# Block 0 with its decodings gathered in one place of a step, GpSimd's part moved, and an attention stage without decodings

## The chip, the cores and the metric

The kernel runs on one core of a Trainium2 chip. TensorE (PE in the profile) multiplies matrices into PSUM; VectorE (DVE), ScalarE (ACT) and GpSimd (POOL) work on tiles; SyncE (SP) issues the transfers. Each engine runs its own instructions strictly in the order in which they were written, and waits on semaphores for what other engines make. The metric is the device time of one execution in microseconds (us).

## The reference

```python
def attention(q, k, v):                      # 8 batches, 8 heads, 576 tokens, head size 64
    q_s = softmax(q, axis=-1)                # exp(q - max) / (sum + 1e-9), over the 64
    k_s = softmax(k, axis=2)                 # the same over the 576 tokens
    return q_s @ (k_s^T @ v)

x = attention(q, k, v)                       # as 4608 tokens x 512
h = x @ w_in;  x = (h - tanh(h)) @ w_out     # 512 -> 2048 -> 512
h = x @ w_in2; x = (P(h) / Q(h)) @ w_out2    # P cubic, Q quadratic in |h|, element by element
```

The four weight matrices come as 64-bit floats, the rest as 32-bit floats.

## The kernel before

The 4608 tokens are handled in nine blocks of 512. For each block, 16 steps make the first feed-forward layer: step f multiplies the block's x by slice f of `w_in` (12 matmuls of 128x512 into the PSUM tile `hps`, three for each of four chunks, because every operand is split in a high and a low part: `xh`, `xl`, `wa..h`, `wa..l`), and two steps later the result by slice f of `w_out` (12 matmuls into `acc`, with `gh`, `gl`, `wb..h`, `wb..l`). There are two `hps` tiles. Between the two products lie, in each step: the tanh on ScalarE (`t`), the subtraction h - tanh(h) on VectorE, which in block 0 writes back into `hps`, the cast to the high part `gh` on ScalarE, and the low part `gl`, in block 0 on VectorE. The second layer's weights are prepared beside the blocks 1 to 8, and the last third of the time is the second layer.

In block 0 two other jobs lie beside the steps.

The first is **decoding**. The weights of the first layer arrive as 64-bit floats in 32 pieces of 128x512 (`a` pieces are `w_in`, `b` pieces `w_out`). A piece is opened (`dec_open`: two ScalarE conversions, of line 131 into `e` and of line 133 into `m`, and one VectorE mask of line 134 into `m`), joined (`dec_join`: a VectorE shift of line 146 on `e` and a VectorE instruction of line 147 that puts the two together in `m`), rounded to its high part on ScalarE (`dec_high`, line 154), and its low part is what is left (`dec_low`, line 158, on VectorE or GpSimd). A piece lies in one of three staging tiles `raw` until it is opened, and the next piece's transfer is issued by SyncE when a staging tile is free. One call of `decode` moves several pieces on by one stage each: a low part, a high part, an opening, a joining of the piece opened a call earlier, and one more fetch. Before, a step of block 0 has two such calls, one between `gh` and `gl`, its low part on VectorE, and one behind the step's attention work, its low part on GpSimd; steps 2 and 6 have one.

The second is the **attention of the next block**: of k the column maxima (`kv_max` into `mx`, transposed by TensorE, `kv_top` into `mc`, transposed back, `kv_sub` into `ke`, `kv_exp`), the product with v (`kv_mm`), its scale (`kv_norm`: two small VectorE instructions on `rs`, then the block diagonal `bd` on ScalarE); of q the row maxima (`q_max` into `qm`), the subtraction on GpSimd (`q_sub` into `qe`), `q_exp`, the sums (`q_sum` into `qs`, then a multiplication on GpSimd), the transpose (`q_turn`, copied out as `qh`), the product with `bd` (`q_mm` into `xps`) and the copies into `xr` (`q_out`, four in a row). A table `work` says which step of block 0 runs which function for which of four head pairs. `front` runs a step's plain functions before the tanh, `turn` the TensorE part of the paired ones, and `follow` their second part behind `gl`.

The attention of block 0 itself stands ahead of the steps, as a pipeline of eight stages `s` over the four head pairs; from stage 2 on each has a decoding as well, the last one two. It ends with `xh` cast by ScalarE and `xl` made by VectorE from the product in PSUM (line 679 and 680).

Of the kernel before, what the change touches and what calls it, by code (L numbers as in the profile page):

```python
# [11 lines left out]
U32 = mybir.dt.uint32  # L12
# [6 lines left out]
P = 128  # L19
NB = 512  # L20
# [23 lines left out]
def attention_moe_moe2_kernel(ctx, tc, q, k, v, w1, w2, w3, w4, ca, cb, out):  # L44
# [12 lines left out]
    NPAIR = H // 2  # L57
# [8 lines left out]
    decp = tc.alloc_tile_pool(name="decp", bufs=2, side="right")  # L66
# [7 lines left out]
    PE, ACT, DVE, POOL, SP = nc.tensor, nc.scalar, nc.vector, nc.gpsimd, nc.sync  # L74

    def f32(ap):
        return ap.bitcast(F32)
# [27 lines left out]
    staged, joining, parting = [], [], []  # L105

    def staging():
        return rawp.tile([P, 2 * NB], F32, tag="raw", name="raw")
# [51 lines left out]
    def dec_start():  # L160

        old = [joining.pop()] if joining else []
        if staged:
            piece, t = staged.pop(0)
            if wide:
                joining.append((piece, t, *dec_open(t)))
            else:
                old.append((piece, t, None, t))
        return old

    def dec_end(ph, old, low_on_dve):
        if parting and parting[0][2]:
            dec_low(*parting.pop(0)[:2], low_on_dve)
        for x in parting:
            dec_high(*x[:2])
            x[2] = True
        if wide:
            for _, _, e, m in old:
                dec_join(e, m)
        parting.extend([piece, m, False] for piece, _, _, m in old)  # L180
        fetch_w(ph)

    def decode(ph, low_on_dve):
        dec_end(ph, dec_start(), low_on_dve)

    parked = {}
    UNITS = (1, 5, 2, 6, 7, 4, 3)
# [149 lines left out]
    def split_low(g, gh, gl, eng):  # L339
        eng.tensor_tensor(out=gl, in0=g, in1=f32(gh), op=ALU.subtract)  # L340
# [322 lines left out]
                    )  # L663
        q_state[j, p] = ps

    def q_out(j, p):
        ps = q_state.pop((j, p))
        if j > 0:
            if j > 1 and p % 2 == 0:
                return  # L670
            n = 2 if j > 1 else 1
            for to in range(2):
                for h, r in enumerate(HEADS):
                    ACT.copy(
                        out=xr[r, p + 1 - n:p + 1, to * HALF:(to + 1) * HALF],
                        in_=ps[h][HEADS[to], 0:n * HALF].rearrange("p (c x) -> p c x", c=n),
                    )
        else:
            ACT.copy(out=xh[:, p, :], in_=ps)
# [5 lines left out]
    def front(todo):  # L685
        for fn, args in todo:
            if not isinstance(fn, tuple):
                fn(*args)

    def turn(todo):  # L690

        got = []
        for fn, args in todo:
            if isinstance(fn, tuple):
                fn[0](*args)
                got.append(lambda fn=fn, args=args: fn[1](*args))
        return got

    def follow(after):
        for fn in [late for fn in after for late in [fn()] if late]:  # L700
            fn()

# [4 lines left out]
    def put(s, fn, *args):  # L707
        work[max(s, 0)].append((fn, args))
# [13 lines left out]
    for j in range(1, NBLK):  # L722
        for p in range(NPAIR):
            if j < B:
                s, at = kv_from[j, p], kv_at[j, p]
                steps = (s - 2, s - 1 - (p == 0), s - (p == 0), s + (p > 0), at) if j == 1 else (s - 3, s - 3, s - 1, s, s, s, at)
                for fn, s in zip(KV if j == 1 else KV_LATER, steps):
                    if fn is not kv_max or (j, p) != (1, 0):
                        put(s, fn, j, p)
            s, at = q_from[j, p], q_at[j, p]  # L730
            steps = (s - 1, s, s + 1, s + 2, at - 2, at) if j == 1 else (s - 1, s, s + 1, s + 2, s + 3, s + 5, at)
            for fn, s in zip(Q if j == 1 else Q_LATER, steps):
                if fn is not q_max or (j, p) != (1, 0):
                    put(s, fn, j, p)
        for p in range(2, NPAIR + 2):
            to, before = (j + p // NPAIR, p % NPAIR), (j + (p - 2) // NPAIR, (p - 2) % NPAIR)
            if to in kv_at:
                put(kv_from[before] + 1, load_k, *to)
                put(kv_at[before] + 1, load_v, *to)
            if to in q_at:  # L740
                put(q_from[before] + 2, load_q, *to)

    with tc.manual_schedule():
# [21 lines left out]
        for s in range(NPAIR + 4):  # L765
            def at(k, *fns):

                return [fn(0, s - k) for fn in fns if 0 <= s - k < NPAIR]

            at(1, kv_turn)  # L770
            at(2, kv_back)
            at(3, kv_mm, q_turn)
            at(4, q_mm)
            at(0, kv_max, q_max, q_sub)
            at(1, q_exp)
            at(1, kv_top)
# [165 lines left out]

        STEPS = NBLK * KF
        PAIRS = STEPS // 2
        due = {}
        last = STEPS - KF
        for n in range(STEPS):
            j, f = n // KF, n % KF
            leave = None
            front(work[n])  # L950
            flush()
            hps = first_product(f)
            if f == KF - 1 and j + 1 < NBLK:
# [4 lines left out]
            if n == last + 10:  # L958
# [16 lines left out]
            if n in due:  # L975
# [5 lines left out]
            after = turn(work[n])  # L981
# [12 lines left out]
            split_low(g, gh, gl, POOL if j else DVE)  # L994
            follow(after)
# [81 lines left out]
```

## Time and profile before

| | us |
|---|---|
| median of three executions (1653.03 to 1655.1) | 1654.87 |
| the profiled execution, its own time | 1656.78 |
| its span, first to last instruction | 1655.0 |
| TensorE busy in the span | 1615.7 |
| VectorE / ScalarE / GpSimd busy in the span | 1109.6 / 1024.5 / 1039.2 |
| first matmul of block 0's steps at | 33.66 |
| first matmul that reads block 1's x at | 140.32 |

The profiled execution lies 1.9 us above the median, and 1.8 us of its own time lie around its span. TensorE's busy time counts overlapping and waiting matmuls alike, so that a full row of it does not say that it was fast. Of a stretch, the starts of the instructions tell more: an engine that works through its queue starts each instruction some 0.1 us before the one ahead of it ends.

### The profile page before, as it was taken

To read this page: it belongs to the slowest core of one execution; us is meant where nothing else is said; L and a number is where in the kernel's file an instruction comes from. 1 tells how busy PE (TensorE), PEld (TensorE's weight loads), DVE (VectorE), ACT (ScalarE), POOL (GpSimd) and SP (SyncE) were. 2 spreads that over 40 slices of the span, in tenths; PEclk is the share of its full clock that TensorE was granted. 3 is DMA by queue.
4 is the path that set the end of the run, shared out by engine and by line. 5 is a ranking of instruction groups with operands and counts; after the bars stand their busy time and mean duration, and the time that the engine had idled before them with its cause. 6 is when DMAs were issued, how large, how long until landed. Compare 5 with 4: busy or idle time off the path is not lost.

```text
span 1655.0 us, 26931 instructions
## 1 busy us (share of the span) xinstructions
PE 1615.7 (98%) x9400; PEld 1375.3 (83%) x9400; DVE 1109.6 (67%) x1839; ACT 1024.5 (62%) x1821; POOL 1039.2 (63%) x876
## 2 busy tenths in 40 slices
PE   5999999999999999999999999999999999999998
PEld 3777888888888888887888989898999999999996
DVE  7997656575565556351214787778787777878786
ACT  6785554544545455443326777777777777777775
POOL 4223727374554637373435888888888877888775
PEclk9999999999999999999999999999999999999999
DMA  8662766666474756351487575858585757676640
GB/s 233 192 182 80 217 175 191 169 186 190 147 208 118 227 150 202 104 174 56 142 305 284 178 281 193 285 189 295 190 297 199 276 195 265 206 252 217 208 139 26
DMA packets 250729, 323.76 MB, mean 196 GB/s; under 512 B 119008, under 2 KB 185568, under 8 KB 241376
## 3 DMA queue, kind: packets, MB, share of 16 engines
q1 hardware_dynamic: 250592, 322.03, 60.9%
q8 instruction: 74, 1.21, 0.3%
q14 instruction: 63, 0.52, 0.1%
HBM read 249.04 MB, written 72.93 MB: 195 GB/s over the span
## 4 chain that ended last, share of the span: by engine, by line
PE 82%; DVE 7%; DMA 3%; ACT 3%; issue 2%; SPq 1%; POOL 1%; DVEq 0%; ACTq 0%; POOLq 0%
PE acc L80 14%; PE acc L81 14%; PE acc L82 14%; PE z L871 12%; PE y L871 9%; PE hps L80 6%; PE hps L81 6%; PE hps L82 6%; DVE m L147 1%; DVE m L134 1%; PE kvps L515 1%; PE xps L660 1%; DMA xh<-x2d 1%; DVE e L146 1%; DVE xl L322 0%
## 5 line engine op out<-in xcount | busy, mean ns | idle before, releaser
L340 POOL TENSOR_TENSOR gl<-t,gh 128x512 fp32r<-128x512 f32 x128 | 174.1, 1360 | 301.0 <-ACT gh L336 278.1
L928 POOL TENSOR_TENSOR n<-n,r 128x512 f32<-128x512 f32 x144 | 186.6, 1296 | 98.2 <-ACT r L925 93.0
L986 DVE TENSOR_TENSOR t<-hps,t 128x512 f32<-128x512 f32 x128 | 88.1, 688 | 233.4 <-ACT t L983 233.4
L336 ACT CAST gh<-t 128x512 fp32r<-128x512 f32 x128 | 79.8, 623 | 248.0 <-PE acc L82 140.5
L928 POOL TENSOR_TENSOR n<-n,n 128x512 f32<-128x512 f32 x144 | 186.7, 1296 | 36.1 <-ACT n L912 36.1
L928 POOL TENSOR_TENSOR n<-n,h 128x512 f32<-128x512 f32 x144 | 187.2, 1300 | 9.7 <-DMA xl<-x2d 9.6
L983 ACT ACTIVATE t<-hps 128x512 f32<-128x512 f32 x144 | 86.0, 597 | 121.0 <-PE hps L82 85.3
L882 ACT COPY sums<-z 128x256 f32<-128x256 f32 x144 | 53.8, 374 | 135.0 <-PE z L871 135.0
L908 ACT ACTIVATE n<-h,coef 128x512 f32<-128x512 f32 x144 | 116.7, 810 | 0.3 <-POOL n L928 0.3
L938 DVE CAST gh<-a 128x512 fp32r<-128x512 f32 x144 | 99.6, 692 | 16.5 <-PE z L871 0.9
L941 DVE TENSOR_TENSOR gl<-a,gh 128x512 fp32r<-128x512 f32 x144 | 99.7, 692 | 15.2 <-DVE gh L938 0.5
L934 DVE SCALAR_TENSOR_TENSOR a<-a,n 128x512 f32<-128x512 f32 x144 | 100.0, 695 | 14.3 <-POOL n L928 8.5
L917 DVE SCALAR_TENSOR_TENSOR a<-h,absb,a 128x512 f32<-128x512 f32 x144 | 107.6, 747 | 3.0 <-ACT a L902 2.9
L902 ACT ACTIVATE a<-h,coef 128x512 f32<-128x512 f32 x144 | 100.5, 698 | 2.7 <-DVE gl L941 2.7
L931 DVE SCALAR_TENSOR_TENSOR a<-a,r 128x512 f32<-128x512 f32 x144 | 99.4, 690 | 0.8 <-ACT r L925 0.8
L920 ACT ACTIVATE r<-a,bias_q 128x512 f32<-128x512 f32 x144 | 97.3, 676 | 0.0
L925 ACT ACTIVATE r<-r 128x512 f32<-128x512 f32 x144 | 91.2, 634 | 4.6
L905 ACT ACTIVATE h<-h 128x512 f32<-128x512 f32 x144 | 89.3, 620 | 0.9 <-DMA xh<-x2d 0.8
L889 DVE TENSOR_TENSOR h<-y,sums 128x256 f32<-128x256 f32 x72 | 30.6, 425 | 58.6 <-PE y L871 58.6
L893 DVE TENSOR_TENSOR h<-y,top 128x512 f32<-128x512 f32 x72 | 49.7, 691 | 27.4 <-ACT top L882 27.1
L613 POOL TENSOR_TENSOR qe<-qe,qs 128x512 f32<-128x512 f32 x36 | 40.6, 1128 | 38.7 <-DVE qs L612 35.4
L80 PE MATMUL acc<-wb3h,gh 128*128 128x512 f32 x144 | 57.0, 396 | 2.9 <-DVE gh L938 2.9
(296 smaller groups left out, 5114.2 us busy)
## 6 DMA issues: line engine op xcount, KB each, us to landing
u<-x2d SPq DMA_DIRECT2D x78, 256.0 KB, 5.5
raw<-in_moe_w_in_dram SPq DMA_DIRECT2D x32, 512.0 KB, 4.8
raw<-in_moe_w_out_dram SPq DMA_DIRECT2D x32, 512.0 KB, 4.1
x2d<-raw SPq DMA_DIRECT2D x64, 256.0 KB, 3.5
x2d<-xr SPq DMA_DIRECT2D x56, 256.0 KB, 3.8
wa0h<-wa0d SPq DMA_DIRECT2D x9, 1024.0 KB, 5.0
wa1h<-wa2d SPq DMA_DIRECT2D x9, 1024.0 KB, 5.0
wa2h<-wa4d SPq DMA_DIRECT2D x9, 1024.0 KB, 5.2
```

Source lines behind the costliest of these rows:

```text
L80: PE.matmul(o, lhi, rhi, start=start, stop=False)
L81: PE.matmul(o, lhi, rlo, start=False, stop=False)
L82: PE.matmul(o, llo, rhi, start=False, stop=stop)
L340: eng.tensor_tensor(out=gl, in0=g, in1=f32(gh), op=ALU.subtract)
L871: PE.matmul(o, w, x[:, xc], start=m in (1, 5) and c == k == 0, stop=c == 1 and k == 2, skip_group_check=True,)
L902: ACT.activation(out=new(t, "a", ps_a), in_=t["h"], func=AF.Abs, scale=b0)
L908: ACT.activation(out=new(t, "n1"), in_=t["h"], func=AF.Identity, scale=a3, bias=a2)
L917: DVE.scalar_tensor_tensor(out=t["a"], in0=t["h2"], scalar=b1, in1=t["a"], op0=ALU.mult, op1=ALU.add)
L928: return lambda t: POOL.tensor_tensor(out=t[a], in0=t[a], in1=t[b], op=op)
L934: DVE.scalar_tensor_tensor(out=t["a"], in0=t["a"], scalar=2.0, in1=t["n0"], op0=ALU.subtract, op1=ALU.mult)
L938: DVE.tensor_copy(out=t["g"][0], in_=t["a"])
L941: DVE.tensor_tensor(out=t["g"][1], in0=t["a"], in1=f32(t["g"][0]), op=ALU.subtract)
```

## The change

It does five things.

1. `dec_start`, `dec_end` and the lists `joining` and `parting` go. A piece now moves through the lists `staged`, `opened`, `joined` and `ready` by four functions: `opens(n)`, `joins(n)`, `highs(n)` and `lows(engines)`.
2. A step of block 0 has one place for VectorE's decoding, behind `gl`: the low part of one piece, two openings, the joining of whatever is opened, and one high part. The other high part stands on ScalarE right behind the tanh, and GpSimd's low part behind that.
3. The attention functions that use VectorE and GpSimd (`BESIDE`) stand between the subtraction and `gl`, and the exponentials (`CLOSING`) at the step's end instead of ahead of its tanh. `kv_top` and the `kv_sub` of a turn move on to the next step.
4. In the attention of block 0, stages 2 to 4 have a decoding; stages 5 to 7 only a few single stages of one. The results of the head pairs 0 and 1 are cast to `xh` by VectorE.
5. The transfers of k for block 1 stand a step later.

```diff
+    def opens(n):
+        for _ in range(min(n, len(staged))):
+            piece, t = staged.pop(0)
+            if wide:
+                opened.append((piece, *dec_open(t)))
...
+            fetch_w(0)
+    def joins(n):
+        for _ in range(min(n, len(opened))):
+            piece, e, m = opened.pop(0)
+            if wide:
                 dec_join(e, m)
+            joined.append((piece, m))
+    def highs(n):
+        for _ in range(min(n, len(joined))):
+            dec_high(*joined[0])
+            ready.append(joined.pop(0))
+    def lows(*engines):
+        for eng in engines[:len(ready)]:
+            dec_low(*ready.pop(0), eng is DVE)
...
+    BESIDE = (kv_max, kv_squares, kv_join, kv_sub, q_max, q_sub, q_sum, q_squares)
+    CLOSING = (kv_exp, q_exp)
...
-            if s < NPAIR + 3:
-                if s >= 2:
-                    decode(0, False)
-                at(5, q_out)
-            else:
+            if 2 <= s <= NPAIR:
+                decode()
+            elif s == NPAIR + 1:
+                lows(POOL)
+                q_out(0, 0, DVE)
+            elif s == NPAIR + 2:
+                highs(1)
+                q_out(0, 1, DVE)
+                lows(POOL)
+            elif s == NPAIR + 3:
+                q_out(0, 2)
+                q_out(0, 3)
+                joins(1)
+                highs(1)
                 kv_max(1, 0)
                 q_max(1, 0)
-                at(5, q_out)
-                at(4, q_out)
-                decode(0, False)
-                decode(0, False)
+                opens(2)
+                lows(DVE)
+                joins(1)
+                fetch_w(0)
...
             ACT.activation(out=t, in_=hps, func=AF.Tanh)
 
             g = t if j else hps
             DVE.tensor_tensor(out=g, in0=hps, in1=t, op=ALU.subtract)
-            ph_w, turns = None, 0
-            if j == 0:
-                ph_w, turns = 0, 1 if f in (2, 6) else 2
+            if not j:
+                highs(2)
+                first = ready[0:1]
+                del ready[0:1]
+                lows(POOL, POOL)
+                follow(beside)
+                only(work[n], BESIDE)
+                if n in due:
+                    due.pop(n)()
+                after = turn(work[n])
+                beside = [x for x in after if x[0] in (kv_top, kv_sub)]
+                after = [x for x in after if x not in beside]
             gh, gl = split_high(g)
             due[n + LAG1] = lambda a=(j, f, gh, gl): second_product1(*a)
-            if turns:
-                decode(ph_w, True)
             split_low(g, gh, gl, POOL if j else DVE)
+            if not j:
+                for x in first:
+                    dec_low(*x, True)
+                opens(2)
+                joins(3)
+                highs(1)
             follow(after)
+            if not j:
+                only(work[n], CLOSING)
             if leave:
                 leave()
-            if turns > 1:
-                decode(ph_w, False)
```

What this does to the order on the engines is seen at three places. The first is VectorE in step 4 of block 0, from its subtraction (`hps`) on; before:

```order
L986 TENSOR_TENSOR hps<-hps,t 128x512
L134 TENSOR_SCALAR m<-raw 128x512
L158 TENSOR_TENSOR wa1l<-m,wa1h 128x512
L146 TENSOR_SCALAR e<-e 128x512
L147 ISA m<-e,m 128x1024
L340 TENSOR_TENSOR gl<-hps,gh 128x512
L520 TENSOR_SCALAR rs<-xps 128x1
L521 RECIPROCAL rs<-rs 128x1
L474 TENSOR_REDUCE mc<-xps 128x1
L134 TENSOR_SCALAR m<-raw 128x512
L146 TENSOR_SCALAR e<-e 128x512
L147 ISA m<-e,m 128x1024
```

and now:

```order
L1011 TENSOR_TENSOR hps<-hps,t 128x512
L348 TENSOR_TENSOR gl<-hps,gh 128x512
L158 TENSOR_TENSOR wa1l<-m,wa1h 128x512
L134 TENSOR_SCALAR m<-raw 128x512 x2
L146 TENSOR_SCALAR e<-e 128x512
L147 ISA m<-e,m 128x1024
L146 TENSOR_SCALAR e<-e 128x512
L147 ISA m<-e,m 128x1024
L528 TENSOR_SCALAR rs<-xps 128x1
L529 RECIPROCAL rs<-rs 128x1
L1011 TENSOR_TENSOR hps<-hps,t 128x512
```

Nothing now stands between the subtraction and `gl`; both masks of line 134 follow the low part of line 158, the two shift-and-join pairs stand one behind the other, `rs` is last before the next subtraction, and `mc` went into step 5.

The second is ScalarE in the same step, from one tanh (`t`) to the next; before:

```order
L983 ACTIVATE t<-hps 128x512
L336 CAST gh<-hps 128x512
L131 ACTIVATE e<-raw 128x512
L133 ACTIVATE m<-raw 128x512
L154 CAST wb1h<-m 128x512
L527 ACTIVATE bd_114<-xps,rs 128x64
L131 ACTIVATE e<-raw 128x512
L133 ACTIVATE m<-raw 128x512
L154 CAST wa1h<-m 128x512
L983 ACTIVATE t<-hps 128x512
```

and now:

```order
L1008 ACTIVATE t<-hps 128x512
L154 CAST wb1h<-m 128x512
L344 CAST gh<-hps 128x512
L131 ACTIVATE e<-raw 128x512
L133 ACTIVATE m<-raw 128x512
L131 ACTIVATE e<-raw 128x512
L133 ACTIVATE m<-raw 128x512
L154 CAST wa1h<-m 128x512
L535 ACTIVATE bd_114<-xps,rs 128x64
L613 ACTIVATE qe<-qe 128x512
L1008 ACTIVATE t<-hps 128x512
```

One high part (`wb1h`) moved from the middle to right behind the tanh; the other (`wa1h`) stands behind all four conversions; `bd` and the exponential of `qe` stand between it and the next tanh.

The third is VectorE in the last stages of block 0's own attention, from the scale (`rs`) of head pair 2 on; before:

```order
L520 TENSOR_SCALAR rs<-kvps 128x1
L521 RECIPROCAL rs<-rs 128x1
L134 TENSOR_SCALAR m<-raw 128x512
L146 TENSOR_SCALAR e<-e 128x512
L147 ISA m<-e,m 128x1024
L680 TENSOR_TENSOR xl<-xps,xh 128x512
L520 TENSOR_SCALAR rs<-kvps 128x1
L521 RECIPROCAL rs<-rs 128x1
L134 TENSOR_SCALAR m<-raw 128x512
L146 TENSOR_SCALAR e<-e 128x512
L147 ISA m<-e,m 128x1024
L680 TENSOR_TENSOR xl<-xps,xh 128x512
```

and now:

```order
L528 TENSOR_SCALAR rs<-kvps 128x1
L529 RECIPROCAL rs<-rs 128x1
L687 CAST xh<-xps 128x512
L688 TENSOR_TENSOR xl<-xps,xh 128x512
L528 TENSOR_SCALAR rs<-kvps 128x1
L529 RECIPROCAL rs<-rs 128x1
L687 CAST xh<-xps 128x512
L688 TENSOR_TENSOR xl<-xps,xh 128x512 x3
L146 TENSOR_SCALAR e<-e 128x512
L147 ISA m<-e,m 128x1024
```

Two whole decodings (masks, shifts and joins) went from here, and two casts to `xh` came in.

## Rows read from the trace of the kernel before

**Rows 1.** Busy time by engine (instructions) from step 0's tanh to step 15's.

```profile
40.49:141.85 101.36, 92.32 (x515) 71.27 (x514) 92.44 (x172) 76.16 (x145) 26.82 (x22) 0.98 0.53 161
```

**Rows 2.** Groups of VectorE in that stretch: busy us, mean ns | idle before.

```profile
L134 DVE TENSOR_SCALAR m<-raw 128x512 uint16<-128x512 uint16 x25 | 17.7, 710 | 0.0
L146 DVE TENSOR_SCALAR e<-e 128x512 uint32<-128x512 uint32 x27 | 13.8, 510 | 0.0
...
L485 DVE TENSOR_TENSOR ke<-kt,kvps 128x640 f32<-128x640 f32 x4 | 3.2, 811 | 0.0
L610 DVE TENSOR_REDUCE qs<-qe 128x8 f32<-128x512 f32 x4 | 2.7, 678 | 0.0
...
L590 DVE TENSOR_REDUCE qm<-qr 128x8 f32<-128x512 f32 x4 | 2.6, 662 | 0.0
```

**Rows 3.** Timeline of VectorE in step 12: start us, us.

```profile
120.10 0.47 DVE L134 TENSOR_SCALAR m<-raw 128x512 uint16<-128x512 uint16 x1
120.44 0.67 DVE L158 TENSOR_TENSOR wb3l<-m,wb3h 128x512 fp32r<-128x512 f32 x1
121.03 0.42 DVE L146 TENSOR_SCALAR e<-e 128x512 uint32<-128x512 uint32 x1
121.49 0.69 DVE L147 CUSTOM_DVE_ANT_0 m<-e,m 128x1024 uint16<-128x1024 uint16 x1
122.10 0.68 DVE L340 TENSOR_TENSOR gl<-hps,gh 128x512 fp32r<-128x512 f32 x1
122.70 1.56 DVE L134 TENSOR_SCALAR m<-raw 128x512 uint16<-128x512 uint16 x1
```

**Rows 4.** Timeline of ScalarE in step 12 (between brackets: idle before, releaser).

```profile
118.87 0.58 ACT L983 ACTIVATE t<-hps 128x512 f32<-128x512 f32 x1
...
121.97 0.60 ACT L154 CAST wa3h<-m 128x512 fp32r<-128x512 f32 x1
122.47 0.59 ACT L624 COPY qh<-qps 128x512 f32<-128x512 f32 x1
```

**Rows 5.** Timeline of VectorE in step 15.

```profile
144.11 0.69 DVE L340 TENSOR_TENSOR gl<-hps,gh 128x512 fp32r<-128x512 f32 x1 [0.71 <-ACT gh L336]
```

**Rows 6.** Groups of ScalarE in the stretch of rows 1.

```profile
L674 ACT COPY xr<-xps 64x256 f32<-64x256 f32 x16 | 5.9, 366 | 0.2
L605 ACT ACTIVATE qe<-qe 128x512 f32<-128x512 f32 x5 | 3.1, 628 | 0.0
L495 ACT ACTIVATE ke<-ke 128x640 f32<-128x640 f32 x4 | 3.0, 744 | 0.0
...
L527 ACT ACTIVATE bd<-xps,rs 128x64 f32<-128x64 f32 x4 | 1.3, 314 | 0.7 <-DVE rs L521 0.6
```

**Rows 7.** One line's VectorE instructions: duration ns min/median/max, first and last start (L457).

```profile
L457 DVE TENSOR_TENSOR mx<-mx,kt x3: 292/293/1016, 59.0 to 99.7; 128x128 f32<-128x128 f32 x3
```

**Rows 8.** The same for L225, a later line, in the blocks behind.

```profile
L225 DVE TENSOR_TENSOR m<-m,e x21: 405/682/1772, 179.7 to 418.8; 128x512 fp32r<-128x512 f32 x18, 128x256 fp32r<-128x256 f32 x3
```

**Rows 9.** Timeline of GpSimd beside the first of rows 7.

```profile
58.84 1.05 POOL L613 TENSOR_TENSOR qe<-qe,qs 128x512 f32<-128x512 f32 x1 [6.47 <-DVE qs L612]
```

**Rows 10.** Timeline of VectorE: the subtractions of steps 2 and 13.

```profile
54.37 0.70 DVE L986 TENSOR_TENSOR hps<-hps,t 128x512 f32<-128x512 f32 x1
...
127.77 0.69 DVE L986 TENSOR_TENSOR hps<-hps,t 128x512 f32<-128x512 f32 x1
```

**Rows 11.** Timeline of TensorE: last value product of the first attention.

```profile
26.84 0.80 PE L515 MATMUL kvps<-vt,ke 128*64 128x65 f32 x20 [1.42 <-ACT ke L495]
```

**Rows 12.** Timeline of TensorE at the end of block 0.

```profile
133.30 0.50 PE L80 MATMUL hps<-xh,wa3h 128*128 128x512 f32 x1
...
138.65 0.39 PE L82 MATMUL acc<-gh,wb3l 128*128 128x512 f32 x1
...
144.90 0.53 PE L82 MATMUL hps<-xh,wa0l 128*128 128x512 f32 x1
```

**Rows 13.** Waits of TensorE from 145 to 1100 us, the longest group.

```profile
PE z L871 <- ACT sums L882: 2.4, 2, 1.9
```

More of the change, by code (lines that the diff above doesn't have):

```diff
@@ L104, in attention_moe_moe2_kernel @@
     ]
-    staged, joining, parting = [], [], []
+    staged, opened, joined, ready = [], [], [], []
     def staging():
@@ L158, in dec_low, with decode @@
         (DVE if on_dve else POOL).tensor_tensor(out=lo, in0=f32(m), in1=f32(hi), op=ALU.subtract)
-    def dec_start():
-        old = [joining.pop()] if joining else []
-        if staged:
+    def opens(n):
+        for _ in range(min(n, len(staged))):
             piece, t = staged.pop(0)
             if wide:
-                joining.append((piece, t, *dec_open(t)))
+                opened.append((piece, *dec_open(t)))
             else:
[L168 to L178, printed above, removed]
-                dec_join(e, m)
[L180 to L184, printed above, removed]
+                m = decp.tile([P, NB], U32, tag="m", name="m", bufs=4)
+                POOL.tensor_copy(out=f32(m), in_=t)
+                opened.append((piece, None, m))
+            fetch_w(0)
[3 more added lines that the diff above has]
+            if wide:
+                dec_join(e, m)
+            joined.append((piece, m))
[6 more added lines that the diff above has]
+            dec_low(*ready.pop(0), eng is DVE)
+    def decode():
+        n, r = len(opened), len(ready)
+        opens(1)
+        lows(*[POOL] * r)
+        highs(1)
+        joins(n)
     parked = {}
@@ L664, in q_mm, with q_out @@
         q_state[j, p] = ps
-    def q_out(j, p):
+    def q_out(j, p, eng=ACT):
         ps = q_state.pop((j, p))
@@ L678, in q_out @@
         else:
-            ACT.copy(out=xh[:, p, :], in_=ps)
+            (ACT.copy if eng is ACT else DVE.tensor_copy)(out=xh[:, p, :], in_=ps)
             DVE.tensor_tensor(out=xl[:, p, :], in0=ps, in1=f32(xh[:, p, :]), op=ALU.subtract)
@@ L683, in attention_moe_moe2_kernel, with front, only @@
     Q_LATER = (q_max, q_sub, q_exp, q_sum, q_squares, q_fetch, (q_mm, q_out))
-    def front(todo):
+    BESIDE = (kv_max, kv_squares, kv_join, kv_sub, q_max, q_sub, q_sum, q_squares)
+    CLOSING = (kv_exp, q_exp)
+    def front(todo, leave=()):
         for fn, args in todo:
-            if not isinstance(fn, tuple):
+            if not isinstance(fn, tuple) and fn not in leave:
+                fn(*args)
+    def only(todo, these):
+        for fn, args in todo:
+            if fn in these:
                 fn(*args)
@@ L695, in turn @@
                 fn[0](*args)
-                got.append(lambda fn=fn, args=args: fn[1](*args))
+                got.append((fn[1], args))
         return got
     def follow(after):
-        for fn in [late for fn in after for late in [fn()] if late]:
-            fn()
+        for fn, args in after:
+            fn(*args)
     work = {s: [] for s in range(NBLK * KF)}
@@ L737, in attention_moe_moe2_kernel @@
             if to in kv_at:
-                put(kv_from[before] + 1, load_k, *to)
+                put(kv_from[before] + (2 if before[0] == 1 else 1), load_k, *to)
                 put(kv_at[before] + 1, load_v, *to)
@@ L944, in attention_moe_moe2_kernel @@
         PAIRS = STEPS // 2
-        due = {}
+        due, beside = {}, []
         last = STEPS - KF
@@ L949, in attention_moe_moe2_kernel @@
             leave = None
-            front(work[n])
+            front(work[n], () if j else BESIDE + CLOSING)
             flush()
@@ L974, in attention_moe_moe2_kernel @@
                     load_unit(0, u)
-            if n in due:
+            if j and n in due:
                 leave = due.pop(n)()
@@ L980, in attention_moe_moe2_kernel @@
                 ring(f // 4 - 1)
-            after = turn(work[n])
+            after = turn(work[n]) if j else []
             t = gp.tile([P, NB], F32, tag="t", name="t", bufs=1)
@@ L986, in attention_moe_moe2_kernel @@
             DVE.tensor_tensor(out=g, in0=hps, in1=t, op=ALU.subtract)
-            ph_w, turns = None, 0
-            if j == 0:
-                ph_w, turns = 0, 1 if f in (2, 6) else 2
+            if not j:
[10 more added lines that the diff above has]
+                after = [x for x in after if x not in beside]
             gh, gl = split_high(g)
             due[n + LAG1] = lambda a=(j, f, gh, gl): second_product1(*a)
-            if turns:
-                decode(ph_w, True)
             split_low(g, gh, gl, POOL if j else DVE)
+            if not j:
[3 more added lines that the diff above has]
+                joins(3)
+                highs(1)
             follow(after)
+            if not j:
+                only(work[n], CLOSING)
             if leave:
                 leave()
-            if turns > 1:
-                decode(ph_w, False)
             if n == KF:
```

## The prediction

> **What bounds it now.** I first asked where a microsecond counts. From 145 us on TensorE hardly waits: the longest group in 955 us is 2.4 us [rows 13]. So whatever block 0 gains or loses until the first product of block 1 ends (its last matmul starts at 144.90 [rows 12]) reaches the end one for one, and nothing behind it changes its order.
>
> In block 0 the stretch from the first tanh to the last takes 101.36 us for 15 steps. VectorE is busy for 92.44 of them, ScalarE for 76.16, GpSimd for 26.82 [rows 1]. TensorE's 92.32 are no measure: at the pace of 133.30 to 138.65 (23 starts in 5.35 us, 0.23 each [rows 12]) the 24 matmuls of a step are worth 5.6 us, 84 for 15 steps, and the attention products some 11 more. VectorE is therefore what sets the step. Part of its time is lost beside GpSimd: a mask takes 0.47 us alone [rows 3] and 0.71 on average, a shift 0.42 and 0.51 [rows 2, 3]; the mask at 122.70 took 1.56. That is 25 x 0.24 + 27 x 0.09 = 8.4 us. The step's own time, from the subtraction of step 2 (54.37) to that of step 13 (127.77) [rows 10], is 73.4 / 11 = 6.67 us.
>
> **The change, part by part.**
>
> *Ahead of the steps.* The last value product of the first attention ends at 27.64 [rows 11], and nothing ahead of it changes. From there the new order is: scale and block diagonal of pair 3, 1.8 us (two small VectorE instructions, four ScalarE ones); its product, 1.0; `xh`, 0.6; `xl`, 0.7; then shift and join of the third piece (0.46 + 0.73 [rows 3]) to 33.1; its high part, 0.5 [rows 4]; four conversions on ScalarE at some 0.6 each, 2.4; tanh and hand-over, 0.62. The first subtraction comes at 36.6. The 1.8, 1.0, 0.6, 0.7 and 2.4 are estimates from instructions of the same size (0.59 to 0.69 for 512 columns [rows 3, 4]). Step 0 joins three pieces and takes 6.5, step 1 takes 5.6 by the chain below, and I add 0.5 because TensorE's transpose for the k maxima now waits for `mc` of step 1: the subtraction of step 2 at 49.2 instead of 54.37, **5.2 us gained**. It costs two pieces that block 0 has to decode in addition.
>
> *A step.* Now the order matters. ScalarE's last high part stands behind all conversions and waits for the first join of the same step; behind it stand the step's closing work and then the tanh, for which VectorE's next subtraction waits. That is a closed chain, with these links from start to start: subtraction to `gl` 1.40 (0.69 and 0.71 of waiting for `gh`, as in step 15 [rows 5], because nothing fills the gap any more); `gl` to the low part 0.60, low part to mask 0.59, two masks 0.69, shift to join 0.46, join to its end and hand-over 0.73 [rows 3]; high part 0.50, tanh with hand-over 0.62 [rows 4]. Sum 5.59, and 61.5 for steps 2 to 12. The second shift and join lie beside the high part and the tanh and cost nothing; without that cover they would cost 1.1 a step. ScalarE's four conversions lie beside `gl`, the low part and the masks.
>
> Attention on VectorE lies between the subtraction and `gl` and is covered up to 0.8 us. Start to start I take 0.72 for `ke`, 0.60 for `qm`, 1.03 for `qs` with its two small ones (their durations in [rows 2], less 0.1 where the next does not depend on it), and as estimates 0.66 for `mx` (0.29 for its second instruction [rows 7], more for the first, which is twice as wide) and 0.34 for `mc`. What exceeds 0.8 is 0.52 in step 2, 0.89 in 3, 1.17 in 5 and 8, 0.58 in 6 and 9, 0.57 in 11: 5.5.
>
> The closing work on ScalarE lies on the chain in full: in steps 2 to 12 four `ke` and four `qe` exponentials, four `qh` copies, eight `xr` copies and three `bd`: 11.7 us by their durations [rows 4, 6], 10.2 from start to start. Before it was hidden: ScalarE had 25 us to spare in the stretch [rows 1] and VectorE did not wait for it. In step 4 `bd` also waits for `rs`, which is behind the second join: 0.9.
>
> So steps 2 to 12 take 61.5 + 5.5 + 11.1 = 78.1 us without any collision, against 73.4: the 8.4 us of collisions go, and 4.7 more than them come in as waits.
>
> *GpSimd beside VectorE.* GpSimd's low part now starts some 0.5 us behind the subtraction and ends 1.3 us later, beside the subtraction and `gl`, which read PSUM. But behind it, in its queue, stand the multiplication of `qe` behind `qs` (1.05 [rows 9]) and the subtraction behind `qm` (1.1 to 1.2, as its neighbour), and these now run beside VectorE's low part, which has both operands in SBUF, or beside `mx`. The trace has VectorE's low part never beside GpSimd, so I bound it: 0 if it doesn't mind, and the rest of the GpSimd instruction if it must wait. For the second speak two near rows: `mx`, which also has two SBUF operands, took 1.016 instead of 0.292 beside the multiplication at 58.84 [rows 7, 9], and L225, a subtraction of the low part's shape, took up to 1.772 against 0.682 [rows 8]. I take the waiting: 0.7 in step 2, 0.5 in 3, 1.05 in 5 and 8, 0.5 in 6, 9 and 11: 4.8, and 0.7 in step 13. The Trainium skill, "SBUF — State Buffer", section "Who interferes with whom", says that a VectorE instruction with two SBUF inputs contends with a GpSimd instruction that reads SBUF, while a reduction never does. The trace agrees in the 1.016 and 1.772 us; by that rule the sum is the one with the 4.8, and sums and `gl` are safe company but the k maxima of block 1 (two `tensor_tensor`) are not.
>
> *The end of block 0.* Step 13 has 2.5 us of attention ahead of `gl`; then low part, one mask, shift, join, high part, four `xr` copies, `bd`: the block diagonal of pair 3 is ready 8.1 us behind the subtraction (0.6 + 2.5 + 0.60 + 0.59 + 0.35 + 0.46 + 0.73 + 0.50 + 1.5 + 0.3). Its product (1.0) and three products of 12 matmuls (35 starts, 8.1) follow without a gap: 17.3 to the last matmul of block 1's first product. Before it was 144.90 - 127.77 = 17.1, with a later wait for `xh` and slow matmuls in it. So +0.2, or +0.9 with GpSimd in the way.
>
> *Sum.* The subtraction of step 13 comes at 49.2 + 78.1 + 4.8 = 132.1 instead of 127.77, +4.3; with the end +5.2, rounded **+5 us**. Without collisions it is -0.3. On the profiled execution's own 1656.78 us this gives 1661.8; on the median, 1.9 lower, **1659.9 us**.
>
> **The rivals.**
>
> *No collisions, the rest as worked out* (or an early start that is 4 us better than I think): -0.3, 1654.6. For it speaks that the order was laid so that GpSimd's low part meets only PSUM readers; against it the queue behind that low part.
>
> *Faster: VectorE keeps its queue full.* Its own work in a step is 0.60 + 0.60 + 0.59 + 0.69 + 2 x 1.08 = 4.6 us; with some 12 of attention and `rs` steps 2 to 12 are 64 us, 14 below the chain. If half of the closing work and of the wait for `gh` is covered after all (conversions finished ahead of time, so that ScalarE reaches high part and tanh early), 7 us come off: 1653 with the collisions, 1648 without. It decides at 6.67 us a step on average: below that, less the 0.5 a step that the early start is worth, the change gains. Against it: the high part stands behind the join in ScalarE's order, and can't be early.
>
> *Slower still: TensorE at a lower rate.* It now stands for a transpose that waits for `mc` in four steps, and ahead of pair 3's product. Block 1's first product before shows the price: it took from 140.32 (the table above) to 144.90 [rows 12], 4.6 us, where 11 starts of 0.23 are 2.6; some 2 us, its wait for `xl` included. If that falls on the three products at the end, +2 to +4: 1662 to 1664.
>
> *The change misses its point.* If the freed collisions are simply taken over by the next queue, without waits, nothing moves: that lies in the first rival's range.
>
> **Chances.** Forecast and lower rate together 0.47, the first rival with its neighbours 0.31, faster 0.22. A difference of 0.2% (3.3 us) is about what a measurement of this kernel tells from none; the forecast lies outside it, the first rival inside. The likeliest case alone is 1657 to 1663; the range, 1648 to 1665, takes in the faster rival without collisions and one slow product with the collisions.
>
> **What would show it.** Right: the first subtraction at 36 to 37 us and TensorE's first product of block 0 some 3 us earlier; ScalarE idle before line 154's high part, released by the join; VectorE idle before the subtraction, released by the tanh, by 10 us or more in block 0, most in steps with `xr` copies; masks at 0.47, but low parts and `mx` of over 1 us. Wrong: a step below 6.2 us on average, a low part of 0.67 us beside GpSimd, or TensorE without waits in block 0.

## The result, and the profile after

The changed kernel takes 1663.26 us in the median of four executions (1662.6 to 1664.21), the kernel before beside it 1654.47: 0.55% slower, ratio 1.0055 with a 95% interval of 1.0037 to 1.0072, +8.8 us. The forecast was 1659.9, the range 1648 to 1665.

The two profiled executions differ by less: spans of 1661.0 and 1655.0. The tanh of step 17 starts at 159.05 instead of 150.99, 8.06 us later; at step 143, the last one, the difference is still 8.41. Most of the missing 2.4 us was lost by the profiled execution of before, later on. Windows of before (first) and after (second) at the passage to the second layer (columns: us, busy us of PE, PEld, DVE, ACT and POOL, granted TensorE clock, DMA share, GB/s):

```profile
860.00:900.00 40.00, 36.60 (x203) 31.98 (x202) 13.43 (x22) 19.68 (x35) 16.05 (x14) 0.96 0.82 312
```

```profile
868.00:908.00 40.00, 36.61 (x211) 31.80 (x211) 13.00 (x21) 20.19 (x37) 15.78 (x14) 1.00 0.82 301
```

Before had 0.96 of the clock in that stretch, after has all of it, which by estimate is worth 40 x 0.04 = 1.6 us of the 2.4; the distance between the two kernels' equal ScalarE instructions falls from 8.42 us (starts 896.74 and 905.16) to 6.91 (908.02 and 914.93) there. Where the rest went was not looked into. So the change's own cost is 8 to 9 us, as the medians say, and all of it arises in block 0.

The stretch from step 0's tanh to step 15's, and eight microseconds near its end, after:

```profile
35.86:148.81 112.95, 93.57 (x502) 72.95 (x501) 92.33 (x177) 81.88 (x150) 28.44 (x23) 0.91 0.51 154
```

```profile
140.00:148.00 8.00, 5.47 (x29) 3.93 (x30) 5.32 (x11) 6.51 (x15) 0.00 (x0) 0.79 0.13 33
```

[rows 1] had 101.36 us with VectorE busy for 92.44. It is busy for the same 92.33 now, but in 112.95 us: 4.6 of the 11.6 that were added are the earlier start, 7.0 the later end, and the whole is waiting. The subtractions of steps 2 and 13 after, to be held against those of [rows 10]:

```profile
49.98 0.70 DVE L1011 TENSOR_TENSOR hps<-hps,t 128x512 f32<-128x512 f32 x1
...
133.93 0.70 DVE L1011 TENSOR_TENSOR hps<-hps,t 128x512 f32<-128x512 f32 x1 [1.13 <-ACT t L1008]
```

VectorE's groups in that stretch (busy us, mean ns, idle before):

```profile
L134 DVE TENSOR_SCALAR m<-raw 128x512 uint16<-128x512 uint16 x27 | 11.6, 485 | 0.0
L146 DVE TENSOR_SCALAR e<-e 128x512 uint32<-128x512 uint32 x28 | 11.6, 415 | 0.0
L1011 DVE TENSOR_TENSOR hps<-hps,t 128x512 f32<-128x512 f32 x15 | 10.5, 699 | 10.2 <-ACT t L1008 10.2
L348 DVE TENSOR_TENSOR gl<-hps,gh 128x512 fp32r<-128x512 f32 x15 | 10.2, 682 | 3.2 <-ACT gh L344 3.1
L158 DVE TENSOR_TENSOR wa3l<-m,wa3h 128x512 fp32r<-128x512 f32 x4 | 3.8, 959 | 0.0
L465 DVE TENSOR_TENSOR mx<-mx,kt 128x128 f32<-128x128 f32 x3 | 3.1, 1017 | 0.1
```

The masks fell from 710 to 485 ns and the shifts from 510 to 415 [rows 2]: those collisions are gone, but for one pair of masks in step 1 that took 1.64 us. In their place VectorE waits 10.2 us for the tanh and 3.1 for `gh`, and the collisions that are left moved to the low parts and `mx`.

The chain behind the 10.2 us, in step 7. ScalarE (first fence) and VectorE (second):

```profile
92.91 0.62 ACT L154 CAST wa2h<-m 128x512 fp32r<-128x512 f32 x1 [0.76 <-DVE m L147]
93.43 1.51 ACT L682 COPY xr<-xps 64x256 f32<-64x256 f32 x4
94.98 0.32 ACT L535 ACTIVATE bd<-xps,rs 128x64 f32<-128x64 f32 x1
95.19 0.62 ACT L613 ACTIVATE qe<-qe 128x512 f32<-128x512 f32 x1
95.71 0.59 ACT L1008 ACTIVATE t<-hps 128x512 f32<-128x512 f32 x1
```

```profile
88.33 0.70 DVE L1011 TENSOR_TENSOR hps<-hps,t 128x512 f32<-128x512 f32 x1 [0.64 <-ACT t L1008]
89.73 0.69 DVE L348 TENSOR_TENSOR gl<-hps,gh 128x512 fp32r<-128x512 f32 x1 [0.71 <-ACT gh L344]
...
92.18 0.69 DVE L147 CUSTOM_DVE_ANT_0 m<-e,m 128x1024 uint16<-128x1024 uint16 x1
...
96.33 0.70 DVE L1011 TENSOR_TENSOR hps<-hps,t 128x512 f32<-128x512 f32 x1 [1.39 <-ACT t L1008]
```

The join that starts at 92.18 releases the high part (`wa2h`); behind it stand four copies, `bd`, an exponential and the tanh, and VectorE's subtraction waits 1.39 us for that. The largest waits of ScalarE for joins, step 0 to 16 (total us, times, longest):

```profile
ACT wa1h L154 <- DVE m L147: 6.5, 4, 3.0
ACT wa2h L154 <- DVE m L147: 6.4, 4, 1.9
ACT wa3h L154 <- DVE m L147: 5.9, 4, 2.4
ACT wb3h L154 <- DVE m L147: 3.8, 1, 3.8
```

### The profile page after: what moved, and what is told of

It reads as the page before. It is cut to its first block, busy times and chain, and to the rows that moved or that the text cites. A ratio compares the mean times of both kernels' runs of the same rounds, so it can differ in the third digit from the quotient of the medians.

```text
span 1661.0 us, 26916 instructions
## 1 busy us (share of the span) xinstructions
PE 1615.2 (97%) x9400; PEld 1375.7 (83%) x9400; DVE 1105.3 (67%) x1842; ACT 1025.4 (62%) x1819; POOL 1038.5 (63%) x875
## 4 chain that ended last, share of the span: by engine, by line
PE 86%; DVE 5%; DMA 4%; ACT 3%; issue 1%; SPq 1%; POOL 0%; DVEq 0%; ACTq 0%; POOLq 0%
PE acc L80 14%; PE acc L81 14%; PE acc L82 14%; PE z L896 12%; PE y L896 9%; PE hps L80 7%; PE hps L81 7%; PE hps L82 7%; DMA u<-x2d 1%; PE kvps L523 1%; PE xps L668 1%; DVE m L147 1%; DMA xh<-x2d 1%; DMA qr<-in_q_dram 0%; DMA raw<-in_moe_w_out_dram 0%
```

## The experiments

Three theories were set against each other. A: the closed chain of join, high part, closing work, tanh and subtraction. B: GpSimd beside VectorE. C: the stages ahead and what they hand on, TensorE's delays with them. One table holds all runs; "steps 2 to 12" runs from the subtraction of step 2 to that of step 13, "end" from there to the tanh of step 17, all from the profiled execution. The first three steps vary by up to 1.7 us between kernels that are the same there, so the medians decide. Each ratio is to the kernel before as it was measured beside that run, with medians from 1653.77 to 1654.47.

| kernel | subtr. 2 | subtr. 13 | steps 2 to 12 | end | median | ratio to before (95%) |
|---|---|---|---|---|---|---|
| before | 54.37 | 127.77 | 73.40 | 23.22 | 1654.47 | |
| after | 49.98 | 133.93 | 83.95 | 25.12 | 1663.26 | 1.0055 (1.0037 to 1.0072) |
| e1_high_free | 52.12 | 130.22 | 78.10 | 22.20 | 1655.81 | 1.0007 (0.9997 to 1.0018) |
| e2_high_last | 50.15 | 131.93 | 81.78 | 22.41 | 1656.37 | 1.0014 (1.0003 to 1.0025) |
| e3_stages_alone | 49.29 | 127.06 | 77.77 | 23.18 | 1652.13 | 0.9988 (0.9975 to 1.0001) |
| e4_steps_alone | 54.59 | 138.75 | 84.16 | 20.87 | 1663.35 | 1.0054 (1.0036 to 1.0072) |
| e5_no_q_gpsimd | 49.78 | 132.43 | 82.65 | 23.73 | 1660.56 | 1.0040 (1.0025 to 1.0055) |
| e6_masks_in_gap | 51.60 | 130.79 | 79.19 | 21.94 | 1656.01 | 1.0008 (0.9998 to 1.0018) |
| e7_rs_early_xr_split | 52.30 | 128.47 | 76.17 | 22.68 | 1652.91 | 0.9992 (0.9982 to 1.0003) |
| e8_lows_on_gpsimd | 52.75 | 131.90 | 79.15 | 22.39 | 1656.54 | 1.0015 (1.0004 to 1.0025) |
| e9_top_in_step_0 | 50.14 | 133.88 | 83.74 | 25.07 | 1662.34 | 1.0053 (1.0040 to 1.0066) |
| e10_rs_early_no_masks | 52.22 | 127.40 | 75.18 | 22.95 | 1652.23 | 0.9991 (0.9983 to 1.0000) |
| e11_best | 47.42 | 121.31 | 73.89 | 23.73 | 1647.01 | 0.9963 (0.9950 to 0.9976) |
| e12_end_high_last | 50.76 | 135.86 | 85.10 | 22.45 | 1660.29 | 1.0042 (1.0029 to 1.0055) |

**e1, the link cut.**

```diff
-                highs(2)
-                first = ready[0:1]
-                del ready[0:1]
+                highs(len(joined) - 1)
...
             gh, gl = split_high(g)
+            if not j:
+                highs(1)
...
-                for x in first:
-                    dec_low(*x, True)
+                lows(DVE)
                 opens(2)
                 joins(3)
-                highs(1)
```

> The changed kernel with one edit: no high part stands at a step's end; both stand behind the next tanh, one ahead of gh (its low part on GpSimd), one behind gh (its low part on VectorE). ScalarE then never waits for a join with the tanh behind it. Theory A (the closed chain join, high part, closing work, tanh, subtraction): the link is cut, VectorE's own order sets the step, 5.6 us and the attention beyond 0.8; steps 2 to 12 fall from 83.95 to 70 to 75 us and the time to 1650 to 1655. Theory B (GpSimd's instructions beside VectorE's make the steps long): those stay, 1661 to 1664. Theory C (the loss lies in the stages ahead and in the work that they hand on): 1661 to 1664.

Steps 2 to 12 fell by 5.85 us, the end by 2.9, the time by 7.4, although the subtraction of step 2 came 2.1 us later. B and C can't be the whole, A holds, but the steps fell by half of what it expected, and the time lies 0.8 us above its range. VectorE in e1, from the end of step 7 to the end of step 8:

```profile
96.37 0.70 DVE L1011 TENSOR_TENSOR hps<-hps,t 128x512 f32<-128x512 f32 x1 [1.39 <-ACT t L1008]
...
102.55 0.69 DVE L147 CUSTOM_DVE_ANT_0 m<-e,m 128x1024 uint16<-128x1024 uint16 x1
103.16 0.69 DVE L1011 TENSOR_TENSOR hps<-hps,t 128x512 f32<-128x512 f32 x1
```

Step 8 ends without a wait: VectorE's own order is the limit there, at 6.79 us, only 0.59 below the chain's 7.38. Step 7 still ends with 1.39 us of waiting, at 7.35 us instead of 8.00: there ScalarE's own row of conversions, copies, `bd` and exponential is almost as long as the chain was (from `gh` at 89.80 to the tanh at 95.75 it pauses for 0.28 us only).

**e2, the closing work off the chain.** The one line `highs(1)` stands behind `only(work[n], CLOSING)`.

> The changed kernel with one line moved: the step's last high part stands behind the closing work, not ahead of it. The join still releases the high part and the tanh still stands behind it; only the closing work (11.1 us in steps 2 to 12) leaves the chain and goes into the time in which ScalarE waits for the join. Theory A: steps 2 to 12 fall by 7 to 10 us, to 74 to 77, and the time to 1653 to 1656. Theories B and C: no change, 1661 to 1664.

The time is 0.4 us above A's range, 6.9 below the changed kernel; steps 2 to 12 are not as A said (-2.2 instead of -7 to -10). The rows and the median don't add up here: the profiled execution, at 1658.71, lies 2.3 us above the median. ScalarE's largest group of waits says what took the place, against 0.9 us in the changed kernel:

```profile
ACT bd L535 <- DVE rs L529: 6.6, 4, 2.7
```

`rs` stands on VectorE behind both joins, so in steps 4, 7, 10 and 13 `bd` waits for it, with the high part and the tanh behind. The end gave 2.7 us, of which e12 tells more.

**e3 and e4, one part alone.** e3 puts the new stages ahead of before's steps (with two decodings in every step), e4 before's stages ahead of the new steps; the lists of pieces are handed over in between.

> One part alone: the first attention's new last stages, with the steps of the kernel before, which now have two decodings in steps 2 and 6 too (the two that left the stages). Theory A: the subtraction of step 0 comes at some 36.5 instead of 41.36, the steps keep 6.67 us, the two additional decodings cost some 2 us each; 0 to 2 us faster than the kernel before, 1653 to 1655. Theory C: the stages are the loss, 1658 or more.

> The other part alone: the steps of the changed kernel behind the first attention's old stages. Theory A: the first subtraction comes at 41.4, the steps take 7.6 us each as in the changed kernel, the last ones a little less because two pieces fewer are left; 1664 to 1668, slower than both kernels. Theory C: 1655 to 1658.

The steps are the whole loss: alone they cost as much as the change. The stages alone bring 2 us in the median, which is not clear of noise (0.9975 to 1.0001). In the profile they are 5.1 us ahead at step 2, and 0.7 are left at step 13, because the two pieces that the stages no longer decode cost 2.6 us in step 2 and 1.7 in step 6. With the new steps they bring nothing, since after and e4 have the same time: 4.8 us ahead at step 13 are given back in an end that is 4.25 longer. After has a mask, a shift and a join in step 13 that e4 has done before, and e4's TensorE has its full clock there (1.00 from 140 to 148 us).

**e5, GpSimd's q instructions left out.**

```diff
-        POOL.tensor_tensor(out=t, in0=t, in1=sm.to_broadcast([P, 8, D]), op=ALU.mult)
+        if j != 1:
+            POOL.tensor_tensor(out=t, in0=t, in1=sm.to_broadcast([P, 8, D]), op=ALU.mult)
```

and the same for the subtraction, with the exponential reading `qr`.

> The changed kernel without GpSimd's two instructions on the q of block 1 (the subtraction of the row maxima and the multiplication by the inverse sums are left out; everything else, VectorE's part too, stays). This is the price of GpSimd beside VectorE in the changed kernel. Theory A (the chain, with 4.8 us of collisions in steps 2 to 12 as predicted): 3 to 5 us less than the changed kernel, 1658 to 1660. Theory B (the collisions are the loss): 8 us or more less, 1655 or below.

2.7 us less, just short of A's range: B falls, and taking these instructions away brings back less than the 4.8 forecast. In step 6 of after, GpSimd (first) and VectorE (second), and VectorE in the same step of e5 (third):

```profile
82.11 1.22 POOL L603 TENSOR_TENSOR qe<-qr,qm 128x512 f32<-128x512 f32 x1
```

```profile
82.46 1.02 DVE L465 TENSOR_TENSOR mx<-mx,kt 128x128 f32<-128x128 f32 x1
```

```profile
81.89 0.29 DVE L465 TENSOR_TENSOR mx<-mx,kt 128x128 f32<-128x128 f32 x1
```

Each collision is there and goes with its GpSimd instruction: steps 3, 6, 9 and 11 get 0.6 to 1.0 us shorter, 2.9 together. But steps 2 and 12 got 0.6 and 0.9 longer (there `gh` waits 1.64 and 1.26 us for TensorE's `acc`), so steps 2 to 12 gain 1.3 in all. The other 1.4 lie in the end, where TensorE kept its clock: `bd` starts 8.53 us behind the subtraction of step 13 in both kernels, but block 1's first product ends 17.66 behind it in e5 and 19.19 in the changed kernel.

**e6, e7, e10: the next limits behind the chain.** e6 is e1 with the two masks in the 0.71 us in which VectorE waits for `gh`; e7 has in addition `rs` behind `gl` and two of the four `xr` copies on VectorE; e10 is e7 with the masks back.

> As e1_high_free, and the two masks stand between the subtraction and gl, where VectorE waits 0.71 us for gh in steps without attention. If VectorE's order now sets the step, steps 4, 7, 10 and the first ones get up to 0.7 us shorter each, 1 to 4 us in all: 1652 to 1655. If ScalarE's order sets just those steps (its row of conversions, xr copies, bd and the exponential of qe in steps 7 and 10), nothing but 1 us: 1655 to 1656.

> As e6_masks_in_gap, and what keeps ScalarE from the tanh in steps 4, 7, 10 and 13 is made shorter: rs stands behind gl instead of behind the joins, and VectorE makes two of the four xr copies. Steps 7 and 10 of e1_high_free had 1.39 us of waiting for the tanh each. Expected: 2 to 5 us less than e6_masks_in_gap, 1648 to 1652. If those steps are set by something else, no change.

> As e7_rs_early_xr_split, with the masks back behind the low part, so that they don't meet GpSimd's low part (pairs of 1.28 to 1.64 us there, 0.80 in e1_high_free) and VectorE waits again 0.7 us for gh in steps without attention. Theory A: both are worth about the same, within 1.5 us of e7_rs_early_xr_split, 1651.5 to 1654.5, and 2 to 4 less than e1_high_free. Theory B: the masks' collisions were the larger part, 2 us or more less than e7_rs_early_xr_split.

e6 gained nothing, 1656.01 against 1655.81, at the edge of the second case of its expectation; e7 gained 3.1 us as expected but lies 0.9 above its stated range, e10 came as expected, and the two are equal. Why masks in the gap bring nothing stands in GpSimd's (first) and VectorE's rows (second) of e7 in step 7:

```profile
87.51 1.57 POOL L158 TENSOR_TENSOR wa2l<-m,wa2h 128x512 fp32r<-128x512 f32 x1 [4.39 <-ACT wa2h L154]
```

```profile
88.46 1.28 DVE L178 TENSOR_SCALAR m<-raw 128x512 uint16<-128x512 uint16 x2
89.63 0.67 DVE L372 TENSOR_TENSOR gl<-hps,gh 128x512 fp32r<-128x512 f32 x1
```

Beside GpSimd's low part the pair takes 1.28 instead of 0.8 us: the gap is paid for in collisions. What brought the 3 us of e7 and e10 is ScalarE's shorter row: the waits for the tanh fell from 7.3 us in e1 to 2.5 and 1.8. How much `rs` and how much the two copies did was not separated.

**e8, both low parts on GpSimd.** One word changed from e7: `lows(POOL)` behind `gl`.

> As e7_rs_early_xr_split, but VectorE's low part goes to GpSimd too, so VectorE has 0.6 us less in each step and GpSimd is beside VectorE for some 1.3 us more. Theory A: 4 to 7 us less than e7_rs_early_xr_split. Theory B: the additional collisions take that back, the same time or more.

3.6 us more than e7 although VectorE has less to do: here B is right. VectorE's groups from 36 to 143 us, e7 and then e8:

```profile
L178 DVE TENSOR_SCALAR m<-raw 128x512 uint16<-128x512 uint16 x27 | 15.3, 614 | 0.8 <-DMA raw<-in_moe_w_out_dram 0.8
L146 DVE TENSOR_SCALAR e<-e 128x512 uint32<-128x512 uint32 x29 | 13.3, 457 | 0.0
```

```profile
L178 DVE TENSOR_SCALAR m<-raw 128x512 uint16<-128x512 uint16 x27 | 18.6, 739 | 0.9 <-DMA raw<-in_moe_w_out_dram 0.9
L146 DVE TENSOR_SCALAR e<-e 128x512 uint32<-128x512 uint32 x29 | 17.5, 604 | 0.9 <-ACT e L190 0.9
```

Masks and shifts together take 7.5 us more. In these runs a low part on GpSimd cost VectorE nothing where it lay beside instructions that read PSUM, or beside sums and maxima made by a reduction.

**e9, the transpose's wait.** `kv_top` of head pair 0 at the end of step 0.

> The changed kernel, where mc of head pair 0 is made at the end of step 0 instead of in step 1, so that TensorE's transpose no longer stands in its queue until step 1's subtraction is done (7.5 us of waiting in the changed kernel). The prediction put 0.5 us on this wait. Theory A (the wait lies beside VectorE's and ScalarE's chain): 0 to 1 us less than the changed kernel, 1662 to 1663.5. Theory C (TensorE, held up in the first steps and slowed after it, is late for the steps behind): 2 us or more less, 1661 or below.

Inconclusive. The edit shortened TensorE's wait from 7.50 to 6.92 us only, because the end of step 0 is hardly earlier than step 1's subtraction. What the wait costs is not shown here; e10 and e11 below say more.

**e12, the end.**

```diff
-                highs(1)
+                if n != 13:
+                    highs(1)
             follow(after)
+            if n == 13:
+                highs(1)
```

> The changed kernel, where in step 13 alone the last high part stands behind the xr copies and bd. There ScalarE waits 3.8 us for the join with these behind it, TensorE waits 2.5 us for them, and its clock is granted at 0.79 in the 8 us behind that wait. If this is what made block 0's end 2 us longer than forecast: bd comes 1.5 to 2 us earlier, the matmuls behind it keep 0.23 us, and 2 to 4 us go: 1659 to 1661. If the end is set by something else: 1662 to 1664.

3.0 us less in the median, 2.1 less than e9, which was measured beside it and is the changed kernel but for the place of one `mc`; the end is 2.7 shorter. After, ScalarE and TensorE behind step 13:

```profile
140.40 0.62 ACT L154 CAST wb3h<-m 128x512 fp32r<-128x512 f32 x1 [3.82 <-DVE m L147]
140.92 1.51 ACT L682 COPY xr<-xps 64x256 f32<-64x256 f32 x4
142.46 0.31 ACT L535 ACTIVATE bd<-xps,rs 128x64 f32<-128x64 f32 x1
```

```profile
142.48 1.51 PE L668 MATMUL xps<-qh,bd 64*64 64x32 f32 x16 [2.52 <-ACT xr L682]
...
144.52 0.63 PE L81 MATMUL hps<-xl,wa3h 128*128 128x512 f32 x1
144.94 0.63 PE L82 MATMUL hps<-xh,wa3l 128*128 128x512 f32 x1
...
153.12 0.39 PE L82 MATMUL hps<-xh,wa0l 128*128 128x512 f32 x1
```

The `xr` copies stand behind the high part that waits for the join, TensorE's product waits for them, and behind its 2.52 us without work it runs at half pace, that of the 1.2 GHz level: starts 0.42 apart instead of 0.23, granted clock 0.79 in the window above. In e12 `bd` starts 6.72 us behind the subtraction instead of 8.53, TensorE does not wait there, and the same window and product read:

```profile
140.00:148.00 8.00, 8.00 (x48) 6.12 (x47) 6.37 (x13) 4.54 (x11) 0.23 (x1) 1.00 0.18 38
```

```profile
142.69 0.98 PE L668 MATMUL xps<-qh,bd 64*64 64x32 f32 x16
```

So e12 takes the longer path and the lower clock away together. The clock alone is told by e5, where `bd` is as late as in the changed kernel: some 1.5 us.

**e11, the sum of what helped.** e10, with `mc` of pair 0 behind step 0's first low part, and `joins(2)` instead of `joins(3)`.

> As e10_rs_early_no_masks, with mc of head pair 0 in step 0 and two joins in step 0 instead of three (the piece left over stays one step behind). Steps 0 and 1 took 15.9 us in e1_high_free and 13.5 in the changed kernel. Expected: 2 to 3 us less than e10_rs_early_no_masks, 1649 to 1652, below the kernel before.

1647.01 us, 0.37% faster than before (0.9963, 0.9950 to 0.9976) and more than was expected. Steps 0 and 1 take 11.4 us instead of the 15.5 of e10. In e7, whose steps 0 and 1 take 15.2, GpSimd (first) and VectorE's third shift and join (second) show where they went:

```profile
42.38 1.56 POOL L158 TENSOR_TENSOR wb0l<-m,wb0h 128x512 fp32r<-128x512 f32 x1 [10.56 <-ACT wb0h L154]
43.91 1.44 POOL L158 TENSOR_TENSOR wa0l<-m,wa0h 128x512 fp32r<-128x512 f32 x1
45.31 1.48 POOL L627 TENSOR_TENSOR qe<-qr,qm 128x512 f32<-128x512 f32 x1
```

```profile
42.74 1.49 DVE L146 TENSOR_SCALAR e<-e 128x512 uint32<-128x512 uint32 x1
44.36 1.53 DVE L147 CUSTOM_DVE_ANT_0 m<-e,m 128x1024 uint16<-128x1024 uint16 x1
```

Two low parts of GpSimd in a row cost a shift and a join some 2 us; e10 has the same two, of 1.49 and 1.53 us. With its third shift and join gone from it, step 0 falls from 8.53 us in e10 to 5.80. Step 1 falls from 7.00 to 5.61, and there the rows of e10 point to the earlier `mc`. ScalarE (first) and VectorE (second) at the end of its step 1:

```profile
51.59 0.60 ACT L1008 ACTIVATE t<-hps 128x512 f32<-128x512 f32 x1 [2.06 <-PE hps L82]
```

```profile
52.22 0.70 DVE L1011 TENSOR_TENSOR hps<-hps,t 128x512 f32<-128x512 f32 x1 [1.35 <-ACT t L1008]
```

TensorE waited 9.4 us for `mc` in e10 and had 0.50 of its clock from 44 to 48 us and 0.62 from there to 52; in e11 it waited 2.9 us, had 1.00 in both stretches, and neither wait above is left. The two edits were not run apart.

## Why the prediction was right, and where it was short

- **The forecast.** +8.8 us came where +5 was forecast: the way and the range were right, but 1663.26 lies just outside what the prediction called the likeliest case alone, 1657 to 1663. Three terms of its sum fell short, the early start by 0.8 us, the steps by 1.05 and the end by 1.2, all to the same side.
- **What bounds it.** Right. The 8.06 us at step 17 are 8.41 at step 143.
- **The early start, 5.2 us.** The first subtraction came at 36.48 (36.6 forecast; its terms add up to 36.45), step 0 took 6.62 (6.5). Step 1 took 6.88 instead of 6.1: GpSimd has two low parts there, not one, and its subtraction behind them made the mask pair 1.64 us. So 4.4 us. What the text named without a price, the two additional pieces, together with the lower clock at the end, makes the start worthless with the new steps (e3, e4).
- **A step, 78.1 without and 82.9 with collisions.** Measured 83.95. The links stood: 1.40 from the subtraction to `gl`, the high part released by the join, the closing work ahead of the tanh. Shift to join was 0.55, not 0.46, some 1.0 over eleven steps; why is open. That the link is the cause is shown by e1. That the closing work costs its 11.1 us is not: cutting it off or cutting the link gives 2 to 6, since VectorE's own order and ScalarE's row stand right behind.
- **Collisions, 4.8.** In the durations they are 4.2 in steps 2 to 12 (`mx` 3.0, low parts 0.8, a small `qs` 0.4), but in other places than forecast: GpSimd's subtraction ran in the next step, beside `mx`, instead of beside the low parts of steps 5 and 8. Those two steps, with 1.05 each in the forecast, have no collision, and steps 3, 6 and 9, with 0.5 each, have 1.1 to 1.3. That the totals agree is partly luck. Some 1.2 of the 4.2 lie beside GpSimd's low parts, which e5 keeps; without its q instructions four steps get back 2.9, and 1.3 are left of that over the steps.
- **The end, +0.2 or +0.9.** This is the term that was furthest out. Block 1's first product ended 19.2 us behind step 13's subtraction (its last matmul starts at 153.12, shown with e12), not 17.3 (the forecast's own terms give 17.2), against 17.1 before: +2.1. The path through high part, `xr` copies and `bd` was right: `bd` is ready 8.84 us behind the subtraction (8.1 forecast, 8.8 with GpSimd in the way). What fell short is what stands behind it: the product with `bd` and the three of 12 matmuls took 10.35 us instead of 9.1, because the first of these matmuls ran at half pace. In e5, with the same path and the full clock, the whole is 17.66. That TensorE runs at a lower rate there was only a rival of the forecast. The rival's 1662 to 1664 is what was measured, but by luck: the lower rate fell on the product with `bd` and the first matmuls behind it, not on three products, and the early start and the steps make up the rest.
- **Sum.** -4.4 + 10.55 + 2.1 = +8.2 us, against the forecast's -5.2 + 9.5 + 0.9 = +5.2.
- **The rule on SBUF.** The Trainium skill, "SBUF — State Buffer", section "Who interferes with whom", as the prediction used it, held in each row: `mx` with two SBUF operands took 1.02 us with GpSimd beside it and 0.29 without (e5), the reduction `qs` 0.68 and `gl`, which reads PSUM, 0.68 in the changed kernel, e1, e8 and e11 alike. Masks and shifts, with one SBUF operand, were slowed too (e7, e8); that the runs show, and the prediction's sentence on it does not cover it.
- **Faster rival.** It asked for 6.67 us a step, less 0.5 for the early start; the sign is wrong, as a start that is 5.2 us early leaves room for steps of up to 7.1. The changed kernel has 7.63. It was right that VectorE can do better, and wrong about how much: with the link cut it needs 6.7 to 7.1 us a step, not 64 us for eleven (63 by its own terms).

## What to carry to other kernels

Before work is gathered in one place of a loop, look at what stands behind the instruction that is released last: an in-order engine carries every wait on to all that is queued behind it, here to the tanh that feeds the next round. Cutting such a link gives back only the distance to the next limit, so look for that limit first. And GpSimd was free help here only beside those VectorE instructions that it did not slow; that, and not its load of 28 us in 113, decided how much work it could take.

## What the runs showed that was not expected

- TensorE without work for 2.52 us fell to half pace (starts 0.42 apart, granted clock 0.79 over 140 to 148 us); in e5, where the same product waited 1.7 us, the clock in that window stayed at 1.00. The length of one wait does not sort the cases, though: the kernel before fell to half pace behind a wait of 1.27 us at 140.32, and kept its clock behind one of 2.08 at 132.31. Its window, and that of e5:

```profile
140.00:148.00 8.00, 7.46 (x24) 5.76 (x25) 6.89 (x12) 3.61 (x7) 0.15 (x1) 0.79 0.12 25
```

```profile
140.00:148.00 8.00, 6.97 (x42) 5.49 (x43) 6.46 (x13) 6.43 (x15) 0.00 (x0) 1.00 0.11 33
```

- A shift and a join of VectorE beside two low parts of GpSimd took 1.49 and 1.53 us instead of 0.42 and 0.69 (e7): the join, too, is slowed.
- When TensorE gets its clock back moves block 0 by whole microseconds. The subtraction of step 3 came at 57.57 in the changed kernel and at 59.26 in e12, whose code is the same up to there and whose VectorE met the same collisions. Both have TensorE wait 7.50 us for `mc` and run at half pace behind it (granted clock 0.58 and 0.50 from 44 to 48 us). Then the changed kernel (first) has its clock again, and e12 (second) not yet; its `gh` of step 2 waits 1.94 us for `acc` instead of 0.87:

```profile
48.00:52.00 4.00, 4.00 (x20) 3.29 (x19) 3.74 (x6) 2.26 (x5) 1.30 (x1) 1.00 0.77 263
```

```profile
48.00:52.00 4.00, 4.00 (x13) 3.17 (x13) 3.25 (x6) 1.72 (x3) 0.69 (x1) 0.67 0.76 258
```
